# Moving loads of x, stage A and weight loads in a fused Fourier-filter and gated-FFN kernel

## The chip, the cores and the metric

One core of one Trainium2 chip. The metric is the device time of one execution in microseconds; the kernel before takes 1022.0 us (median of the first three runs, 1019.55 to 1022.17). Engine names in the profile: PE is TensorE's matmuls, PEld its weight loads, DVE is VectorE, ACT is ScalarE, POOL is GpSimd, SP is SyncE; a `q` behind a name is that engine's own queue of DMA issues. A transfer is issued when its queue sends it off, and it has landed when what waits for it may start. The DMA share is the mean busy share of the core's 16 DMA engines; a share times the length of a stretch is called engine time here.

## The reference

```python
# x: (8, 3008, 256) f32; filters: (1505, 256); FFN: 256 -> 1536 -> 256
X = np.fft.rfft(x, axis=1)
y = np.fft.irfft(X * (filt_r + 1j * filt_i)[None], n=3008, axis=1)
h = y.reshape(8 * 3008, 256)
out = (np.maximum(h @ w_gate, 0.0) * (h @ w_val)) @ w_out
```

## The kernel before

The transform over 3008 = 94 x 32 points is done as matmuls in stages, per batch b:

- **stage A** (`psA`): DFT over 94 points, x from `XF` (two halves, XF_89 and XF_90), 16 items of 512 columns. Its result must change which index lies on partitions, so it goes through DRAM: stored to `Abuf`, read back as `at`. I call this the **A bounce**.
- **filter stage** (`items_b`): `psX` (DFT over 32 points), two products with the filters, `psD` (inverse). Stored to `Dbuf`, read back as `dC`: the **D bounce**.
- **psY** (inverse over 94 points), then the FFN: psV and psG (value and gate), `prod`, psO.

Blocks of 512 tokens run through the FFN in 12 steps each; the stages of later batches are woven in as side items at chosen steps. Batch 0 and most of batch 1 have to be done ahead of or at the start of that loop. The parts that the change touches:

```python
def load_x(b, eng, cut=None): ...            # 3 DMAs per half of XF
...
load_x(0, nc.sync, 2 * q)
...
for i, f in enumerate(items_a(0)):           # stage A of batch 0
    f(); warm(1, 256)                        # warm: matmuls on junk, to keep the clock up
    if i == 0: load_tables()
    ...
load_x(1, nc.sync)
early = items_a(1)
def amid(i):                                 # inside filter stage of batch 0, 12 steps
    if i < 5: warm(1)
    else: next(early)()
for f in items_b(0, amid): f()
load_vg(DFF // 3, DFF)                       # rest of the gate and value weights, GpSimd queue
load_d(0, 0, 2)                              # first two dC
hold_gpsimd(dCs[0, 0][0:32, 0, 0:8])         # GpSimd waits for dC here
load_o()
for i in range(5):
    next(early)(); warm(1, 256)
...
for b in range(1, B):                        # main loop, recorded at steps
    # s0: first stage-A step of batch b; sb0 = s0 + 24 or so: first filter step
    ...
    for c in range(4):
        at_step(s0 + n - 10 + 4 * c if b > 1 else 4, lambda b=b, c=c: load_at(b, c))
    if b + 1 < B:
        at_step(s0 + n + 1, lambda b=b: load_x(b + 1, nc.gpsimd))     # n = 16
```

## Time and profile before

| | |
|---|---|
| time | 1022.0 us |
| PE busy | 962.5 us, 94% of the span of 1021.4 us |
| PE waits on `at` of batches 0 and 1 | 7.5 and 12.3 us |
| PE waits on `at` of batches 3 to 6 | 5.1, 3.6, 2.4, 3.4 us |
| first psX of batch 1 | at 106.95 us |

The page's second part shows where this lies. Here are the rows of TensorE, of the clock that it was granted and of the DMA engines, in tenths, over 40 equal slices of the span:

```profile
PE   8566899999999989998999999999899999999996
PEclk9689899999999989999999999999999999999999
DMA  9969124164143521535124542335515142241111
```

The holes of PE are in the first five slices (128 us); later ones are shallow. The DMA engines are busy for 90% or more of the first, second and fourth slice, and for 60% of the third (51 to 77 us). So the opening is where transfers hold up the kernel, and afterwards it is TensorE, but for four short waits.

### The profile page before, as it was taken

What the parts mean: (1) busy time and instruction counts of PE and PEld (TensorE: products, weight loads), DVE (VectorE), ACT (ScalarE), POOL (GpSimd) and SP (SyncE); (2) the same over time, 40 slices, a digit from 0 to 9 for tenths busy, and PEclk for the clock granted to TensorE, in tenths of its full rate; (3) what the DMA queues carried; (4) which work ended last, traced back from release to release, by engine and by line L of the source; (5) the groups of instructions that cost most, each with busy time, mean ns of one, the idle gap of its engine ahead of it and who ended that gap; (6) DMA issues with size and microseconds to landing.
All of it is one profiled execution on the core that took longest, in us unless ns stands there. A gap on an engine that the chain in (4) does not pass through costs nothing.

```text
span 1021.4 us, 16241 instructions
## 1 busy us (share of the span) xinstructions
PE 962.5 (94%) x6010; PEld 568.1 (56%) x6010; DVE 544.8 (53%) x821; ACT 527.9 (52%) x942; POOL 44.0 (4%) x72
## 2 busy tenths in 40 slices
PE   8566899999999989998999999999899999999996
PEld 3233566556665556654666456655566556666664
DVE  4323675437753467534765348653575437755552
ACT  4353455555555545554555545555455555555552
POOL 4230000010000000000000000000000000000000
PEclk9689899999999989999999999999999999999999
DMA  9969124164143521535124542335515142241111
GB/s 260 246 166 258 43 65 104 46 178 121 55 113 105 165 63 54 115 126 166 38 78 94 157 133 61 87 71 151 135 54 124 47 107 62 61 109 39 35 31 43
DMA packets 94400, 106.29 MB, mean 104 GB/s; under 512 B 7764, under 2 KB 84692, under 8 KB 92628
## 3 DMA queue, kind: packets, MB, share of 16 engines
q1 hardware_dynamic: 87712, 81.34, 30.6%
q0 software_dynamic: 6208, 22.71, 8.0%
q8 instruction: 47, 0.77, 0.3%
q10 hardware_dynamic: 400, 1.20, 0.3%
q14 instruction: 33, 0.27, 0.1%
HBM read 59.32 MB, written 49.81 MB: 107 GB/s over the span
## 4 chain that ended last, share of the span: by engine, by line
PE 85%; DMA 13%; ACT 1%; POOL 0%; SPq 0%; issue 0%; DVE 0%; ACTq 0%; POOLq 0%
PE psV L352 22%; PE psG L352 22%; PE psO L370 22%; PE psA L239 10%; PE psY L336 2%; PE psX L271 2%; PE psD L291 2%; PE psD L290 2%; DMA Abuf_72<-asb 1%; DMA XF_89<-in_x_dram 1%; DMA Abuf_74<-asb 1%; DMA Abuf_75<-asb 1%; DMA Abuf_77<-asb 1%; DMA Abuf_76<-asb 1%; DMA XF_90<-in_x_dram 1%; DMA Dbuf_80<-dsb 1%
## 5 line engine op out<-in xcount | busy, mean ns | idle before, releaser
L357 DVE SCALAR_TENSOR_TENSOR prod<-psG,vsb 128x512 bf16<-128x512 f32 x564 | 389.9, 691 | 376.3 <-ACT vsb L355 361.7
L355 ACT CAST vsb<-psV 128x512 bf16<-128x512 f32 x564 | 331.3, 587 | 248.4 <-PE psV L352 218.4
L370 PE MATMUL psO<-WoT,prod 128*128 128x256 bf16 x2256 | 339.5, 274 | 2.5 <-ACT osb L376 2.5
L352 PE MATMUL psV<-yT,WvT 128*128 128x512 bf16 x1128 | 339.9, 383 | 0.5 <-DVE yT L343 0.3
L352 PE MATMUL psG<-yT,WgT 128*128 128x512 bf16 x1128 | 339.0, 382 | 0.0
L370 PEld LDWEIGHTS <-prod 128*128 128x128 bf16 x2256 | 222.0, 98 | 148.9 <-issue 6.4
L352 PEld LDWEIGHTS <-WgT 128*128 128x128 bf16 x1128 | 110.9, 98 | 136.9 <-issue 5.9
L352 PEld LDWEIGHTS <-WvT 128*128 128x128 bf16 x1128 | 104.9, 99 | 60.4 <-issue 50.0
L242 ACT CAST asb<-psA 96x512 bf16<-96x512 f32 x128 | 74.2, 582 | 114.4 <-PE psA L239 109.9
L274 DVE TENSOR_TENSOR tt<-psX,Ftr 128x512 bf16<-128x512 f32 x96 | 65.4, 682 | 42.9 <-PE psX L271 42.7
L293 ACT CAST dsb<-psD 128x512 bf16<-128x512 f32 x96 | 56.2, 587 | 53.3 <-PE psD L291 51.6
L376 ACT COPY osb<-psO 128x512 f32<-128x512 f32 (+1 forms) x96 | 55.4, 577 | 33.6 <-PE psO L370 28.2
L271 PE MATMUL psX<-at,F_92 128*128 128x256 bf16 x192 | 38.3, 283 | 34.3 <-DMA at<-Abuf_72 12.3
L239 PE MATMUL psA<-XF_89,WA 128*96 128x512 f32 x128 | 66.9, 607 | 3.5 <-DMA XF_89<-in_x_dram 3.5
L239 PE MATMUL psA<-XF_90,WA 128*96 128x512 f32 x128 | 65.8, 600 | 0.8 <-DMA XF_90<-in_x_dram 0.8
L280 DVE TENSOR_TENSOR uu<-psX,Fti 128x512 bf16<-128x512 f32 x88 | 59.9, 680 | 0.0
L291 PE MATMUL psD<-uu,I2u 128*128 128x256 bf16 x192 | 48.2, 277 | 0.8 <-POOL uu L278 0.8
L290 PE MATMUL psD<-tt,I2t 128*128 128x256 bf16 x192 | 48.4, 278 | 0.0
L336 PEld LDWEIGHTS <-dC 96*128 96x128 bf16 x604 | 35.8, 100 | 20.6 <-issue 10.4
L336 PE MATMUL psY<-M_91,dC 96*128 96x94 bf16 (+18 forms) x604 | 39.1, 203 | 6.6 <-DMA dC<-Dbuf_80 6.5
L343 DVE CAST yT<-psY 128x512 bf16<-128x512 f32 x47 | 32.2, 684 | 24.4 <-PE psY L336 24.4
L341 ACT CAST yT<-psY 128x512 bf16<-128x512 f32 x47 | 27.5, 586 | 26.5 <-PE psY L336 26.4
(48 smaller groups left out, 191.1 us busy)
## 6 DMA issues: line engine op xcount, KB each, us to landing
XF_89<-in_x_dram POOLq DMA_DIRECT2D x17, 512.0 KB, 6.1
XF_90<-in_x_dram POOLq DMA_DIRECT2D x17, 512.0 KB, 9.1
out_dram<-osb SPq DMA_DIRECT2D x72, 94.0 KB
XF_90<-in_x_dram SPq DMA_DIRECT2D x6, 512.0 KB
XF_89<-in_x_dram SPq DMA_DIRECT2D x6, 256.0 KB
Abuf_71<-asb SPq DMA_DIRECT2D x4, 384.0 KB
at<-Abuf_71 SPq DMA_DIRECT2D x4, 384.0 KB
XF_89<-in_x_dram SPq DMA_DIRECT2D x3, 512.0 KB
```

The source lines that it names most:

```text
L239: nc.tensor.matmul(psA[0:NROW], WA[:, :NROW], XF[c * NC2 // NX2][:, o:o + 512], start=True, stop=True)
L242: nc.scalar.copy(dst, psA[0:NROW])
L271: nc.tensor.matmul(psX[:, i], F2[:, g + i, :], at[:, g + i, :], start=True, stop=True)
L274: nc.vector.tensor_tensor(tt, psX, Ftr[:, g:g + 2, :], op=ALU.mult)
L280: nc.vector.tensor_tensor(uu, psX, Fti[:, g:g + 2, :], op=ALU.mult)
L290: nc.tensor.matmul(psD[:, i], I2t[:, g + i, :], tt[:, i], start=True, stop=False)
L291: nc.tensor.matmul(psD[:, i], I2u[:, g + i, :], uu[:, i], start=False, stop=True)
L336: nc.tensor.matmul(psY[:, o:o + w], dCs[b, n2 // 4][:, n2 % 4, h * 128:(h + 1) * 128], M1[:, n1:n1 + w], start=True, stop=True)
L352: nc.tensor.matmul(pt[:, :W], w[:, h, ft * 128:(ft + 1) * 128], yt[:, h, :], start=(h == 0), stop=(h == 1))
L355: nc.scalar.copy(vsb, psV[:, :W])
L357: nc.vector.scalar_tensor_tensor(prod, in0=psG[:, :W], scalar=0.0, in1=vsb, op0=ALU.max, op1=ALU.mult)
L370: nc.tensor.matmul(psO[:, t % 2], prods[ft][:, t * 128:(t + 1) * 128], WoT[:, ft, :], start=(ft == 0), stop=(ft == NFT - 1))
```

## The change

Its intent: keep loads of x from running beside the stores and loads of the two bounces; issue the first x from two engines; give the D bounce of batch 0 more of stage A of batch 1 to hide behind; give GpSimd six of batch 0's filter products instead of eight, and not the last one; and let the big weight loads wait until the last D store has landed (a one-row load from `Dbuf` on GpSimd's queue, which must wait for that store, stands ahead of them).

```diff
-    load_x(0, nc.sync, 2 * q)
+    load_x(0, (nc.scalar, nc.sync), 2 * q)          # DMAs go to the two in turn
...
-        if i == 0:
+        if i == 4:
             load_tables()
...
-    POOL_G = (2, 4)
+    POOL_G = (2, 4, 8, 10, 14, 18)
...
-            if b == 0 and g % 6 in POOL_G:
+            if b == 0 and g in POOL_G:
...
     def amid(i):
-        if i < 5:
+        if i < 8:
             warm(1)
...
+    load_d(0, 0, 2)
+    nc.gpsimd.dma_start(pro.tile([1, D], BF16, tag="last", bufs=1, name="last"),
+                        _ap(Dbuf[0], (N2 * NROW - 1) * D, [[D, 1], [1, D]]))
     load_vg(DFF // 3, DFF)
-    load_d(0, 0, 2)
-    hold_gpsimd(dCs[0, 0][0:32, 0, 0:8])
     load_o()
-    for i in range(5):
+    for i in range(8):
         next(early)()
...
-            at_step(s0 + n + 1, lambda b=b: load_x(b + 1, nc.gpsimd))
+            at_step(sb0 + 3, lambda b=b: load_x(b + 1, (nc.gpsimd,)))
```

More of the change, by code (lines that the diff above doesn't have):

```diff
@@ L150, with load_x @@
     WoT = consts.tile([128, NFT, D], BF16)
-    def load_x(b, eng, cut=None):
+    def load_x(b, engs, cut=None):
         w = NX2 * D
+        n = 0
         for c, xf in enumerate(XF):
@@ L158, in load_x @@
                     rows = min(32, B * N1 - (b * N1 + 32 * m))
-                    eng.dma_start(xf[m:m + 4 * rows - 3:4, c0:c1],
-                                  _ap(x, (b * N1 + 32 * m) * N2 * D + c * w + c0,
-                                      [[N2 * D, rows], [1, c1 - c0]]))
+                    n += 1
+                    engs[n % len(engs)].dma_start(xf[m:m + 4 * rows - 3:4, c0:c1],
+                                                  _ap(x, (b * N1 + 32 * m) * N2 * D + c * w + c0,
+                                                      [[N2 * D, rows], [1, c1 - c0]]))
     H = NG // 2
@@ L426 @@
     nc.sync.dma_start(gate, ats[0][96:128, NG - 1, 0:8])
-    load_x(1, nc.sync)
+    load_x(1, (nc.sync,))
     early = items_a(1)
     def amid(i):
-        if i < 5:
+        if i < 8:
             warm(1)
```

## The prediction

> **What bounds the kernel now.** I read the page first, then TensorE's waits (PE in the views), then the chain of waits with its times, then the DMA queues by stretch. On the page TensorE is busy for most of the span:
>
> ```profile
> PE 962.5 (94%) x6010; PEld 568.1 (56%) x6010; DVE 544.8 (53%) x821; ACT 527.9 (52%) x942; POOL 44.0 (4%) x72
> ```
>
> So only what TensorE stands still for, or runs at a lower clock for, can be won. Its waits by cause, from the view of waits:
>
> ```profile
> PE psX L271 <- DMA at<-Abuf_72: 12.3, 1, 12.3
> ...
> PE psX L271 <- DMA at<-Abuf_71: 7.5, 1, 7.5
> ...
> PE psY L336 <- DMA dC<-Dbuf_80: 6.5, 1, 6.5
> ...
> PE psX L271 <- DMA at<-Abuf_74: 5.1, 1, 5.1
> ```
>
> (us in total, times, longest.) `Abuf` and `Dbuf` are the two DRAM bounces: stage A stores to Abuf and reads it back as `at`; the inverse stage stores to Dbuf, read back as `dC`. The waits on `at` of batches 4 to 6 add 3.6, 2.4 and 3.4 us, the first x of batch 1 another 3.5. Batches 0 and 1 thus wait 29.8 us, batches 3 to 6 14.5. The chain shows the prologue's two last waits (start us, us, what):
>
> ```profile
> 62.60 7.70 DMA Dbuf_80<-dsb
> 70.73 3.07 DMA dC<-Dbuf_80
> ...
> 84.87 15.04 DMA Abuf_72<-asb
> 99.98 6.92 DMA at<-Abuf_72
> 106.95 0.61 PE psX L271 x2
> ```
>
> From 106.95 on TensorE is the bound except in the four later waits, so **the new time is the old one plus the shift of this first psX of batch 1, plus whatever happens to those four waits**. What holds that psX is bytes, not one late instruction (columns: stretch; its length; busy us of PE, PEld, DVE, ACT, POOL; clock; DMA share; GB/s):
>
> ```profile
> 71.00:107.00 36.00, 20.81 (x97) 9.39 (x98) 10.88 (x16) 11.30 (x20) 4.96 (x9) 0.78 1.00 231
> ```
>
> The 16 DMA engines are full for all 36 us, and TensorE is busy for only 20.8 of them.
>
> **What the Trainium skill says.** "DMA: Bandwidth & Descriptors", section "Issuing engines are not separate DMA queues": DMAs of all issuers interleave on the same 16 engines; a second issuer saves only issue time. The trace agrees: the share stands at 1.06 over 4 to 32 us, with three issuers. Same page, "Queues, rings and completion order": each engine goes round the queues packet by packet. The trace fits: the last A store of batch 3, issued beside 1.5 MB of x on another queue, took 12.2 us to land, that of batch 7, with no x beside it, 5.4. "TensorE: Matmul & The Clock Gate", "Part 1: The HAM clock gate": after an idle window of about 3.4 us the clock is halved until a busy one. The trace has 0.50 after each wait and pairs of psV matmuls at 0.85 us instead of 0.43.
>
> **The change, part by part.**
>
> (1) *First x on two queues, tables later.* Issue of the first six x pieces took SyncE 3.77 us (2.03 on); two issuers halve that. But TensorE's first stage-A matmul at 8.16 stood behind 14 warm-up matmuls (5.79 us), which stay, and 4 to 32 us is DMA-full. What may go is the 0.8 us wait for XF_90. Stage A ends 0.5 to 1 us earlier, and `at` of batch 0 lands near 36.2 instead of 37. Tables are issued at item 4 instead of 0, about 4 us later: VectorE places them from 22 on instead of 18.3, is done about 33 to 35, still before 36. Worth about 0.8.
>
> (2) *Stage A of batch 1 starts at step 8 of batch 0's filter stage instead of 5.* Before, steps 0 to 4 ran 37.06 to 43.3, then a matmul waited 3.5 us for x until 46.84, and the pause put the clock at 0.50 until about 52. Now: 36.2 + 6.2 = 42.4; steps 5 to 7 with a warm-up matmul cost about 1.0 each (two psX 0.21 + 0.43 + four psD 0.43 = 0.86 at full clock; VectorE 0.61 to 0.69 per product) = 45.4; x lands 9.6 us after the gate as before, 45.8, so the wait nearly vanishes. Four steps with stage A take 1.51 each (the pitch of 54 to 59 us) = 51.8; the last two inversions 1.5 = 53.3; copy and issue 0.9 = 54.2. Before it was 62.60: **8.4 us earlier**. Of these about 2 are three stage-A matmuls taken out (0.86 - 0.21 each), 3.5 the wait, 2.7 the slow clock.
>
> The Pool list now has 6 members instead of 8: VectorE gets two more products, 1.3 us, spread over steps where it has slack; at the end no Pool product (1.16) has to be awaited (0.8).
>
> (3) *Weights wait for the last D store.* Its landing took 8.1 us beside 2 MB of weights. With nothing beside it the last D stores of batches 1 to 7 are waited for only 2.0 to 4.8 us in SyncE's waits; I take 4.0: landed at 58.2 instead of 70.7, dC at 61.3 instead of 73.8. TensorE fills that with 8 stage-A items of 0.97 (7.8 us, 53.3 to 61.1), so it does not cool. **First psY 12 us earlier.**
>
> (4) *What (3) gives back.* The same weights now lie behind the D store, in the full stretch. Their cost in engine time from the queue view:
>
> ```profile
> q0 software_dynamic: 531, 1.03, 62.8%
> ```
>
> This is 61 to 71 us: 62.8% of 10 us = 6.3 us of all engines. So from D landed to `at` of batch 1 landed it takes 36.2 (70.7 to 106.9) + 6.3 = 42.5 us: 58.2 + 42.5 = 100.7. A part of x of batch 2 may now trail `at`; I allow 1 us. **psX of batch 1 at 99.7: 7.3 us earlier.** Also ft 4 of block 0 needs the late weights: first psV near 62.5, four steps of 1.72 = 69.4, weights issued near 59.3 and landing 9 to 14 us later (8.0 to 14.1 measured), so a new wait of 0 to 4 us on the gate or value weights. TensorE reaches step 13 near 87 in any case and then waits on `at`, so this wait should cost nothing.
>
> (5) *x of batch b+1 recorded at sb0 + 3 instead of s0 + 17.* The lists of both built programs show GpSimd's queue with nothing but these loads in the main loop, in the same order, each half waiting for the same thing: the last stage-A matmul of that half (and older DMAs long landed). Recording later does not make a queue wait longer. The trace shows that it does not wait for the recorded step even now: XF_89 of batch 4 goes out at 326.23, as its eighth stage-A item ends, long before step s0 + 17. And XF_90 at
>
> ```profile
> 344.01 1.57 POOL L159 DMA_DIRECT2D XF_90<-in_x_dram  x3 [16.21 <-PE psA L239]
> ```
>
> beside the A store at 344.36, which lands 12.17 later. So the four later waits (14.5 us, and about 9 us more for 3 to 6 us each at half clock) stay. **Worth 0**, though it is what the change is named for.
>
> Sum: 7.3 us, mostly from (2) and (3), with (1) in it. 1022.0 - 7.3 = 1014.7; I take 1014, since the slow clock after a shorter wait may shrink by half a microsecond.
>
> **Rivals.**
>
> *R1: x really moves.* If the four waits vanished, 14.5 + about 9 = 23 us more would go: about 991. For: the title, and batch 7 without x waits for nothing. Against: the waits of the built queue are the same. Chance 5%.
>
> *R2: the bytes are not the bound in the A bounce.* If `at` landed as soon as TensorE reaches step 13 (87), the gain would be 20 us: 1002. For: TensorE's idle time is there. Against: share 1.00 over 36 us. A partial form, x yielding to `at`, would give 1008 to 1010.
>
> *R3: contention eats all.* If the late weights slow dC and the A stores by more than their bytes (the round-robin between queues; x of batch 2 took 15.0 us to land already), psX of batch 1 stays near 105 and the time near 1020. For: GpSimd's queue is now longer by 2 MB.
>
> *R4: luck in the later batches.* Batch 2 has the same x beside its A store but this landed in 5.9 us, since it got in between two x pieces, and had no wait. If one of five batches changes sides, that is 5 to 8 us either way.
>
> **Range and chances.** The sum's parts are good to about 2 us at D landed (x landing, D store) and 4 in the A bounce; with R4 one side in four. That makes 1005 to 1020. Faster by over 2% needs under 1001.6, so R1 or a full R2: 7%. Slower by over 2% needs 1042, for which I see no cause: 1%.
>
> **What will show it.** First psA on XF_90 without a wait, `at` of batch 0 landing 36 to 37. No wait for XF_89 near 46; last D store issued 53 to 56, landed within 5 us; weights issued just after; first psY 60 to 63 with TensorE busy until then at full clock. A possible wait of psV or psG on WvT or WgT. psX of batch 1 still waiting on `at`, until 97 to 102, with the DMA share near 1.0. XF loads of batches 3 to 7 as now, within 0.5 us of the last stage-A matmul, and waits of psX of 2 to 5 us in batches 3 to 6. Wrong if: those waits are gone (R1), psX of batch 1 starts under 93 (R2) or over 104 (R3).

## The result

1015.49 us (median of 4 runs, 1013.92 to 1017.75) against 1022.09 (1019.55 to 1023.17, 4 runs). The ratio is 0.9941, 95% interval 0.9914 to 0.9968. A ratio here is the mean time of one kernel's fast runs over the mean of the other's fast runs of the same rounds, so it is not quite the ratio of the medians quoted. Faster by 0.6%.

TensorE's waits of the kernel after, from the view of waits (us in total, times, longest):

```profile
PE psX L273 <- DMA at<-Abuf: 38.2, 6, 15.6
PE psA L241 <- DMA XF<-in_x_dram: 2.7, 1, 2.7
...
PE psG L354 <- DMA WgT<-in_moe_w_gate_dram: 0.6, 1, 0.6
```

Six waits on `at` as before. By stretch they are 7.7 and 15.6 us for batches 0 and 1, and 4.8, 2.9, 2.4, 4.8 for batches 3 to 6: the later four add to 14.9 us, against 14.5 before. The wait for dC (6.5 us before) is gone, and the gate weights are waited for 0.6 us. Next, SyncE's queue around the D bounce (start, duration of the issue, source line), the first dC of the kernel before and then the kernel after:

```profile
70.35 0.89 SPq L314 DMA_DIRECT2D dC<-Dbuf_80  x2
```

```profile
55.99 0.82 SPq L297 DMA_DIRECT2D Dbuf<-dsb  x2
59.29 0.85 SPq L316 DMA_DIRECT2D dC<-Dbuf  x2
60.20 4.07 SPq L246 DMA_DIRECT2D Abuf<-asb  x2
```

The first dC can only go out once the last D store has landed: 59.29, against 70.35 before, 11.1 us earlier. The chain of waits shows how much of that reached the end of the opening:

```profile
72.50 17.71 DMA Abuf<-asb
90.28 8.02 DMA at<-Abuf
98.34 0.60 PE psX L273 x2
```

The first psX of batch 1 starts at 98.34 instead of 106.95, 8.6 us earlier (two later runs with the same opening, e1 and e4, have it at 96.98 and 97.22, so a single trace is good to some 1.4 us); the last A store in front of it now takes 17.71 us to land, against 15.04. From dC's issue to this psX it is 39.05 us (36.6 before), and the DMA share is no lower than it was (columns as in the stretch of the prediction, DMA share and GB/s last):

```profile
60.00:98.30 38.30, 21.13 (x105) 9.55 (x105) 10.88 (x16) 13.48 (x25) 6.39 (x11) 0.83 1.07 243
```

The profiled spans differ by 7.4 us (1021.4 and 1014.0), so of the 8.6 us about one is lost again later, and the four later waits differ by 0.4 of it.

### The profile page after: what moved, and what is told of

Same layout as the page of the kernel before. It is cut to its first block, busy times and chain, and to the rows that moved or that the text cites. A ratio compares the mean times of both kernels' runs of the same rounds, so it can differ in the third digit from the quotient of the medians.

```text
span 1014.0 us, 16145 instructions
## 1 busy us (share of the span) xinstructions
PE 951.2 (94%) x5906; PEld 566.4 (56%) x6016; DVE 546.2 (54%) x823; ACT 527.0 (52%) x940; POOL 42.0 (4%) x70
## 4 chain that ended last, share of the span: by engine, by line
PE 85%; DMA 11%; issue 1%; DVE 1%; ACT 1%; SPq 0%; POOL 0%; ACTq 0%
PE psG L354 22%; PE psO L372 22%; PE psV L354 21%; PE psA L241 10%; DMA Abuf<-asb 7%; DMA at<-Abuf 3%; PE psX L273 2%; PE psD L293 2%; PE psD L292 2%; PE psY L338 2%; DMA XF<-in_x_dram 1%; DMA out_dram<-osb 1%; ACT vsb L357 0%; DVE prod L359 0%; PE psJ L391 0%
## 5 line engine op out<-in xcount | busy, mean ns | idle before, releaser
L354 PE MATMUL psG<-yT,WgT 128*128 128x512 bf16 x1098 | 331.4, 381 | 4.4 <-DMA WgT<-in_moe_w_gate_dram 0.6
L354 PE MATMUL psV<-yT,WvT 128*128 128x512 bf16 x1049 | 321.7, 382 | 1.7 <-ACT yT L343 0.6
L241 PE MATMUL psA<-XF,WA 128*96 128x512 f32 x256 | 129.6, 592 | 2.7 <-DMA XF<-in_x_dram 2.7
L273 PE MATMUL psX<-at,F 128*128 128x256 bf16 x192 | 38.5, 284 | 39.1 <-DMA at<-Abuf 38.2
L161 POOL DMA_DIRECT2D XF<-in_x_dram x36 | 19.0, 532 | 625.6 <-PE psA L241 625.4
L273 PEld LDWEIGHTS <-F 128*128 128x128 bf16 x192 | 18.9, 100 | 43.9 <-issue 25.6
L338 PEld LDWEIGHTS <-dC 96*128 96x128 bf16 x604 | 35.3, 99 | 13.5 <-issue 10.8
L241 PEld LDWEIGHTS psA<-XF,WA 128*96 128x96 f32 x256 | 35.1, 163 | 12.2 <-issue 5.9
L345 DVE CAST yT<-psY 128x512 bf16<-128x512 f32 x47 | 32.2, 685 | 17.8 <-PE psY L338 17.8
```

The source lines that it names most:

```text
L241: nc.tensor.matmul(psA[0:NROW], WA[:, :NROW], XF[c * NC2 // NX2][:, o:o + 512], start=True, stop=True)
L273: nc.tensor.matmul(psX[:, i], F2[:, g + i, :], at[:, g + i, :], start=True, stop=True)
L354: nc.tensor.matmul(pt[:, :W], w[:, h, ft * 128:(ft + 1) * 128], yt[:, h, :], start=(h == 0), stop=(h == 1))
```

## The experiments

The open question is the part that the change is named for: did moving the loads of x do anything, and would it if they really moved? GpSimd's queue in the kernel after, beside the A store of batch 3 in the chain:

```profile
337.04 1.57 POOL L161 DMA_DIRECT2D XF<-in_x_dram  x3 [16.21 <-PE psA L241]
```

```profile
337.39 12.09 DMA Abuf<-asb
```

Just as before (344.01, and 12.17 us for the store at 344.36), the load of the second half of x goes out 0.35 us ahead of the last A store, as soon as stage A has read that half. Three theories were at stake: (T1) recording a load later does nothing, because GpSimd's queue holds nothing else and waits only for stage A; (T2) a load that truly waits would clear the later waits; (T3) in the A bounce of batch 1 the bytes of x are what delays `at`.

**e1: undo the move.**

```diff
-            at_step(sb0 + 3, lambda b=b: load_x(b + 1, (nc.gpsimd,)))
+            at_step(s0 + n + 1, lambda b=b: load_x(b + 1, (nc.gpsimd,)))
```

> The changed kernel with one part undone: loads of x of batch b+1 recorded at s0+n+1 again instead of sb0+3. Theory (recording later does not make an in-order queue wait longer): same time as the changed kernel, 1015.5 within 3 us (ratio to before 0.991 to 0.997), same four waits of psX on at, about 15 us together. Rival (the move does clear the bounces): slower than the changed kernel by 3 us or more.

Measured: 1014.04 us (1012.74 to 1015.76), ratio 0.9922 [0.9901, 0.9943]; the changed kernel had 0.9941 [0.9914, 0.9968]. The four later waits are there too (4.7, 2.8, 2.4 and 3.3 us in its trace, 13.2 together; the view puts the first of these psX waits down to a store of `out`), and the load goes out at the same point, when stage A has read that half:

```profile
335.94 1.57 POOL L161 DMA_DIRECT2D XF<-in_x_dram  x3 [16.21 <-PE psA L241]
```

The move is worth nothing that can be measured; T1 holds.

**e2, e3, e4: make x wait.** A small copy on GpSimd that reads `at` from all partitions stands ahead of the loads in GpSimd's queue, so that x goes out only after all four pieces of `at` have landed (the two lines of GpSimd further down show it). e2 does it for all batches, e3 only for x of batch 2, e4 only for x of batches 3 to 7.

```diff
-            at_step(sb0 + 3, lambda b=b: load_x(b + 1, (nc.gpsimd,)))
+            def held_x(b=b):
+                if True:                     # e3: b == 1;  e4: b > 1
+                    xh = sb.tile([128, 8], BF16, tag="xh", bufs=2, name="xh")
+                    nc.gpsimd.tensor_copy(xh, ats[b][:, NG - 1, 0:8])
+                load_x(b + 1, (nc.gpsimd,))
+            at_step(sb0 + 3, held_x)
```

What I expected of e2, e3 and e4, in this order:

> The changed kernel, with a small GpSimd copy from all partitions of at ahead of each load of x of batch b+1, so that these loads really wait until at of batch b has landed. Theory: the four later waits (14.9 us) go, with about 8 us of half clock behind them, and 12 us of engine time of x of batch 2 leaves the A bounce of batch 1, whose wait falls from 15.6 to about 4: 1015.5 - 23 - 12 = about 980 (975 to 990). Rival (x is not what slows the bounce; small packets of at and dC are): under 8 us faster, 1008 or more. Second rival: x then collides with the D stores and a wait on dC or on x appears.

> Only x of batch 2 held until at of batch 1 has landed. Theory (bytes bound the A bounce of batch 1, x costs 12 of its 38 us): first psX of batch 1 near 87 instead of 98.3, wait 4 us instead of 15.6, time about 1004; the four later waits stay. Rival (the bounce is bound by its own stores and loads of small rows): psX at 95 or later, time 1012 to 1016.

> Only x of batches 3 to 7 held until at of the batch before has landed. Theory: the last A stores of batches 3 to 6 land in 5 to 6 us instead of 10 to 12, no wait of psX on at there, clock 1.0: about 23 us less, 992. psX of batch 1 stays at 98.3. Rival: waits shrink only by part, 1003 or more.

| kernel | median us | ratio to before | first psX of batch 1 |
|---|---|---|---|
| after | 1015.49 | 0.9941 [0.9914, 0.9968] | 98.34 |
| e3, x of batch 2 held | 1005.92 | 0.9835 [0.981, 0.9861] | 89.94 |
| e4, x of batches 3 to 7 held | 992.42 | 0.9712 [0.9691, 0.9734] | 97.22 |
| e2, all held | 983.61 | 0.9625 [0.9603, 0.9646] | 88.07 |

All three went the way that T2 and T3 say, and they add: 9.6 + 23.1 = 32.7 us for e3 and e4 against 31.9 for e2. In e2 the waits on `at` are those of batches 0 and 1 alone:

```profile
PE psX L273 <- DMA at<-Abuf: 15.2, 2, 7.9
```

How the wait of batch 4 went, in SyncE's queue, first the kernel after, then e2:

```profile
463.00 0.46 SPq L246 DMA_DIRECT2D Abuf<-asb  x1
473.29 0.32 SPq L260 DMA_DIRECT2D at<-Abuf  x1
```

```profile
444.98 0.46 SPq L246 DMA_DIRECT2D Abuf<-asb  x1
451.00 0.32 SPq L260 DMA_DIRECT2D at<-Abuf  x1
```

The last piece of `at` is loaded once the last A store has landed: 10.3 us after the store's issue with x beside it, 6.0 without. And in e2 GpSimd's queue shows the hold and x behind it:

```profile
454.94 0.18 POOL L476 COPY xh<-at 128x8 bf16<-128x8 bf16 x1 [113.19 <-DMA at<-Abuf]
455.45 3.15 POOL L161 DMA_DIRECT2D XF<-in_x_dram  x6 [0.33 <-PE psY L338]
```

No wait on x or dC appeared in the later batches, so the second rival of e2 is out. In size T3 was off: I had expected the A bounce of batch 1 to shrink by the 12 us that I took x to cost in engine time. From dC's issue to psX it took 31.2 us in e2 and 32.2 in e3, against 39.05: about 7 to 8 us less. TensorE still waited 7.9 us there, so it was not TensorE that stopped the gain. The 12 was wrong: GpSimd's queue over just this stretch, first the kernel after (59.29 to 98.34, 39.05 us), then e2 (56.91 to 88.07, 31.16 us), shows (packets, MB, share of the engines)

```profile
q0 software_dynamic: 2432, 4.98, 52.4%
```

```profile
q0 software_dynamic: 2144, 1.84, 38.9%
```

which is 20.5 and 12.1 us of engine time, so x cost 8.4 us, close to the 7.9 us that the stretch became shorter. That x's presence is what delays `at` is shown; whether it does so by its bytes alone or also by the turns that the queues take is not separated by these runs.

**e5, e6: the first x.** In the trace of the kernel after, stage A of batch 0 waited 2.7 us for the second half of x (0.8 before) and psX of batch 0 started at 38.76 (37.06 before). e5 puts the first x back on one queue, e6 puts the tables back to item 0:

```diff
-    load_x(0, (nc.scalar, nc.sync), 2 * q)       # e5
+    load_x(0, (nc.sync,), 2 * q)
...
-        if i == 4:                               # e6
+        if i == 0:
             load_tables()
```

What I expected of e5 and e6:

> The changed kernel with the first x on SyncE alone again, tables still at item 4. In the changed kernel the ninth stage-A matmul of batch 0 waited 2.7 us for the second half of x (0.8 before) and at of batch 0 landed at 38.5 (36.8 before), where I had expected 36.2. Theory (two queues land the first half sooner, so the filters start sooner, 7.0 instead of 7.9, and both halves then share the engines with them and arrive later): wait back to under 1 us, psX of batch 0 near 37, time 1 to 2 us under the changed kernel. Rival (the wait has to do with the tables' later issue): wait stays near 2.7.

> The changed kernel with the tables issued at item 0 again, first x still on two queues. Theory (tables at item 0 only add to what x shares the engines with): wait for the second half of x 2.7 us or more, psX of batch 0 at 38.5 or later, time within 2 us of the changed kernel or slower. Rival (the later tables delay the last A store of batch 0): psX of batch 0 near 37.

Measured: e5 1012.81 us (1010.47 to 1015.16), 0.9907 [0.9882, 0.9932]; e6 1015.15 us, 0.9929 [0.9909, 0.9949]. The intervals overlap with each other and with that of the kernel after. In e5 the wait was gone and psX of batch 0 started at 37.26, as expected; but in e6 it started at 36.91, so my theory for e6 failed in its trace. One trace of this opening settles nothing here, since it is not so repeatable: with the same opening as the kernel after, psX of batch 0 started at 36.99 (e1), 36.36 (e2), 37.71 (e3) and 37.31 (e4), so 38.76 was the late end of a spread of 2.4 us, and no effect can be read from it. e9 below asks again on a steadier base.

**e7, e8: one part alone on the kernel before.** e7 has only the stage-A items moved (8 and 8 for 5 and 5), e8 only the weights behind the last D store (both hunks are in the diff of the change above).

What I expected of e7 and e8:

> The kernel before with only the stage-A items of batch 1 moved (from step 8 of the filter stage, 8 instead of 5 afterwards). Theory: last D store issued about 5 to 8 us earlier than 62.6, but still lands beside the weights, since these go out after the last Pool product, which also comes earlier: landed near 63 to 65 instead of 70.7, psX of batch 1 about 6 us earlier than 106.95; time about 1016. Rival (the gain needs the weights' wait too): under 2 us, 1020 or more.

> The kernel before with only the weights' wait for the last D store. Theory: D landed 4 us earlier (66.7), but the weights' 6.3 us of engine time move into the A bounce of batch 1: psX of batch 1 at 107 to 110, time 1021 to 1025, no gain by itself. Rival (clearing the D bounce is worth its 4 us): psX near 103, time 1018.

| kernel | median us | ratio to before | dC issued | first psX of batch 1 | between |
|---|---|---|---|---|---|
| before | 1022.0 | 1 | 70.35 | 106.95 | 36.6 |
| e7, stage A moved | 1017.38 | 0.9956 [0.993, 0.9982] | 64.88 | 100.22 | 35.3 |
| e8, weights later | 1018.89 | 0.9974 [0.9952, 0.9996] | 62.84 | 102.01 | 39.2 |
| after, both and the rest | 1015.49 | 0.9941 [0.9914, 0.9968] | 59.29 | 98.34 | 39.05 |

e7 came out as expected. For e8 the theory failed and the rival was right: dC went out 7.5 us earlier, not 4 (the last D store was issued 1.5 us earlier, at 61.10, and landed in 1.7 us instead of 7.7), and the late weights made the A bounce 2.6 us longer, not 6.3. So moving the weights gives a little by itself. The intervals of e7, e8 and the kernel after overlap; which part carries how much is read from medians and single traces. The shorter Pool list had no run of its own; from psX of batch 0 to the issue of the last D store it took 18.1 us in e7, with the old list, and 17.6 in the kernel after.

**e9, e10, e11, e12: parts on top of the held x.** e2's four runs lie within 0.7 us (983.27 to 983.91), a better base for small parts than the kernel before (1019 to 1026 over its runs). e9 is e2 with the first x and the tables as before; e10 is e2 with the weights as before; e11 is e2 with stage A of batch 1 as before; e12 is the kernel before with the held x alone (recorded at sb0 + 3). The edits are those shown. What I expected, in this order:

> On top of e2_hold_all (983.6, its runs within 0.7 us, so a good base for small parts): first x on SyncE alone and tables at item 0 again, as in the kernel before. Theory (4 to 32 us is full for the DMA engines either way, the first psX of batch 0 varied by 2.4 us between traces of the same prologue): within 1.5 us of 983.6. Rival (two queues and later tables are worth their 0.8 us or more): 984.5 or more. Second rival (they cost): 982 or less.

> On top of e2_hold_all: weights issued before the last D store again, as in the kernel before. Theory from e7 (D landed 7 us later than with the weights behind it, A bounce 5 us shorter): first psY 7 us later, and since the A bounce is now shorter than what TensorE has to do before step 13, psX of batch 1 is late by 2 to 5 us: 986 to 989. Rival (the two cancel): 983 to 985.

> On top of e2_hold_all: stage A of batch 1 from step 5 again, 5 instead of 8 items in the D bounce. Theory: D landed 5 to 6 us later (62.8 in e8 against 57), psX of batch 1 as much later: 988 to 990. Rival (its gain is hidden behind at): under 985.

> The kernel before with the held x loads alone, no other part of the change. Theory: the four later waits and their slow clock go (23), and the A bounce of batch 1 loses 12 us of x: 1022 - 35 = 987 (984 to 992). Rival (before, the D bounce holds everything so that x of batch 2 matters less): 996 or more.

| kernel | median us (range) | ratio to before | first psX of batch 1 |
|---|---|---|---|
| e2 | 983.61 (983.27 to 983.91) | 0.9625 [0.9603, 0.9646] | 88.07 |
| e9, first x as before | 983.44 (983.27 to 984.99) | 0.9619 [0.9601, 0.9636] | 88.04 |
| e10, weights as before | 984.3 (983.25 to 988.31) | 0.9631 [0.9608, 0.9654] | 91.03 |
| e11, stage A as before | 989.09 (986.62 to 991.29) | 0.9668 [0.9647, 0.969] | 95.15 |
| e12, only the held x | 987.48 (985.86 to 992.03) | 0.9659 [0.9636, 0.9682] | 93.79 |

e9 to e12 ran on another chip than e2, so differences under 1 us between e2 and these are not to be read. First x and tables: nothing. Stage A: 5.5 us. Weights: 0.7 us in the medians, inside the spread of e10, so not my theory (986 to 989) but its rival; yet in the traces e10's psX came 3.0 us later than e2's. Where that went is seen in TensorE's timeline of batch 1, first e2, then e10 (in brackets the wait before):

```profile
88.07 0.61 PE L273 MATMUL psX<-at,F 128*128 128x256 bf16 x2 [7.90 <-DMA at<-Abuf]
93.40 0.38 PE L273 MATMUL psX<-at,F 128*128 128x256 bf16 x2
```

```profile
91.03 0.39 PE L273 MATMUL psX<-at,F 128*128 128x256 bf16 x2 [2.98 <-DMA at<-Abuf]
93.86 0.38 PE L273 MATMUL psX<-at,F 128*128 128x256 bf16 x2
```

The first pair of psX takes 0.61 us in e2 and 0.39 in e10: after its wait of 7.9 us e2 ran at half clock (0.50 over 88 to 92 us) and e10, after 3.0 us, did not (1.00 over 91 to 95). At the second psX the two are 0.4 to 0.5 us apart. A later start after a shorter wait can be as good as an earlier start after a longer one. e12 is the cheapest of all: holding x on the kernel before gives 34.8 us, five times what the whole change gave. In its trace TensorE hardly waits for `at` of batch 1 any more:

```profile
93.79 0.39 PE L271 MATMUL psX<-at,F 128*128 128x256 bf16 x2 [2.27 <-DMA at<-Abuf]
```

Put together, the traces tell what x of batch 2 and the late weights cost in the A bounce of batch 1 (us from dC's issue to the first psX):

| | x of batch 2 beside it | x held |
|---|---|---|
| weights ahead of the last D store | 36.6 (before), 35.3 (e7) | 25.8 (e12), 27.2 (e10) |
| weights behind it | 39.2 (e8), 39.05 (after), 39.5 (e1), 39.7 (e4) | 32.2 (e3), 31.2 (e2), 31.0 (e11), 30.9 (e9) |

In pairs that differ in little else the weights make it 2.6 us (e8 less before), 3.7 (after less e7), 4.0 (e2 less e10) and 5.2 us (e11 less e12) longer. x makes it 10.8 (before less e12), 8.2 (e7 less e10), 8.1 (e8 less e11) and 7.9 us (after less e2) longer. These are differences of single traces.

## Why the prediction was right

The time (1014 foretold, 1015.5 measured) lies in the range, and the mechanism behind it holds: the opening became shorter by stage A and the D store, the A bounce gave part of it back, and the four later waits stayed. That the number came so close is partly luck, since the terms erred in opposite ways: D landed 1.1 us later than told (59.29 for 58.2), the A bounce was 2.4 us shorter (39.05 for 41.5), and about 1 us of the earlier psX was lost later. Two of the signs told did not show in this trace: the first psA on XF_90 waited 2.7 us, and `at` of batch 0 landed at 38.5.

- *(1) First x and tables, 0.8 us.* Not there: e9 shows no gain, and the spread of 2.4 us in psX of batch 0 hides anything smaller in single traces. The DMA share from 4 to 32 us is 1.06 before and 1.06 after, which fits the reason given for expecting little; 0.8 was still too much.
- *(2) Stage A of batch 1.* From psX of batch 0 to the last D store I had 18.0 us (36.2 to 54.2). Measured: 38.76 to some 56.4, 17.6. Right in length, late in start. By the medians of e7 (4.6 us of 6.6) and e11 (5.5 us) this part carries most of the gain.
- *(3) The D store lands alone.* I took 4.0 us for it; from 56.4 to 59.29 it is 2.9, and in e8 1.7. The prediction read the landing before as 8.1 us, to 70.7, where the chain has 7.70, to 70.30. The wait for dC on TensorE went, as told.
- *(4) What is given back.* The term of the sum that was mis-sized: 6.3 us of engine time for the late weights, of which I let 5.3 count (41.5 us from D landed to psX). Measured 39.05, so 2.4 more than before, and 3.7 more than e7, which has stage A in the same place; e8 alone gave 2.6. The step that failed is the adding of engine time to a stretch taken as full at a share of 1.00: over this stretch the share was 0.99 before and 1.05 after, in e2 it stood at 1.25 over 70 to 80 us, and the prediction itself quotes 1.06 for 4 to 32 us, so 1.00 was no ceiling. (The queue view counts these weights as 1.03 MB, the 16-bit form in which they land; the 2 MB of the prediction is their 32-bit source.) The wait on the gate weights was in range (0.6 us).
- *(5) The recorded step of x, worth 0.* Shown by e1, and its other half, that loads which really wait would be worth much, by e4 (23.1 us; R1's figure was 23) and e2. The four later waits stayed as foretold (14.9 us for 14.5). One reading in the prediction is off: the 5.4 us for the last A store of batch 7 is SyncE's wait for it; from its issue (839.60) to the load behind it (845.31) it is 5.7.
- *Rivals.* R1 is out for this change. R2 and R3 are out: psX of batch 1 at 98.34 is neither under 93 nor over 104, and it still waited on `at`. R4, luck in a single batch, did not occur in this trace: the waits were in the same four batches.

What stays open: why the late weights, 6.3 us of engine time in the kernel before and 5.6 in the kernel after (20.5 of its queue less 14.9 of e7's), lengthen the A bounce by 2.6 us in one pair of traces and by 5.2 in another. Nor is it all a matter of full engines: in e2 TensorE waited for `at` over 84 to 88 us at a share of 0.76. No run here takes this apart.

## What to carry to other kernels

When a load sits on a queue with nothing else in it, moving the line that records it changes nothing; look at what its queue waits for, and if it should go out later, put something ahead of it that has to wait. A prefetch that goes out the moment its buffer comes free can meet the store made from that very buffer, as here in batches 3 to 6: delay the prefetch until the critical round trip is over, as long as there is time left for it (here some 70 us: in e2 x of batch 5 is loaded from 455 us on and first read at 528). A DMA share near 1.0 hints at what bounds a stretch, but engine time taken from another stretch can misstate what one transfer costs there; measure it by holding the transfer back.

## What the Trainium skill lacked or had wrong

- "DMA: Bandwidth & Descriptors", "Queues, rings and completion order", tells of the round robin by packets; it lacks what this costs a small transfer beside a large one: the last A store of batches 3 to 6, 384 KB, landed in 9.8 to 12.1 us beside 1.5 MB of x, and in 5.7 to 7.8 us with x held back. (The statement of its section "Issuing engines are not separate DMA queues" that a second issuer saves only issue time held: 983.44 us with one queue for the first x, tables moved too, 983.61 with two.)
- "TensorE: Matmul & The Clock Gate", "Part 1: The HAM clock gate", names an idle window of about 3.4 us for the halved clock, and calls the window free-running. Here a wait of 2.4 us in the kernel before (batch 5, to 607.59) was followed by 0.50 over 609 to 611 us, while waits of 2.4 us in the kernel after (batch 5), 3.0 us in e10 and 2.3 us in e12 were followed by 1.00. A free-running window would account for equal waits that end differently; how idle a window has to be, so that a wait shorter than one is followed by the halved clock, the page does not say.
- "Perfetto Trace Analysis", "Identifying the Most-Contended Engine", calls the occupancy of the 16 DMA engines misleading, but no page tells what a transfer costs that is added where the share is near 1.0. Here the share stayed at 0.99 to 1.06 from dC's issue to the first psX of batch 1 in every run, while the stretch took 25.8 to 40.1 us by what was loaded in it; weights of 5.6 to 6.3 us of engine time made it 2.6 to 5.2 us longer.
